# Q and K of the first two tiles on 32-column tiles of TensorE, in an adaLN transformer block on one core

## The chip, the cores and the metric

One Trainium2 chip, one of its cores. The metric is the device time of one execution in microseconds (us), lower is better. A core has TensorE (PE) for matmuls, with its weight loads shown as PEld; VectorE (DVE), ScalarE (ACT) and GpSimd (POOL) for elementwise work; and SyncE (SP), whose queue issues almost all DMAs here. Each engine runs its own instructions strictly in the order in which the program emits them.

## The reference

The input `x` has 2048 rows of 448 numbers (bf16). A vector `c` gives six modulation vectors. Then an attention over a dilated sliding window (8 keys, every second row, 16 heads of 28) and an MLP of 1792 follow, each with its own layernorm, modulation and gate:

```python
mod = (_silu(c) @ w_mod).reshape(c.shape[0], 6, 1, -1)
sa, ca, ga, sb, cb, gb = (mod[:, 0], mod[:, 1], mod[:, 2], mod[:, 3], mod[:, 4], mod[:, 5])
h = _layernorm(x) * (1 + ca) + sa
x = x + ga * _A_ref(h, A_wqkv, A_wo)          # qkv = h @ wqkv; window attention; @ wo
h = _layernorm(x) * (1 + cb) + sb
x = x + gb * _B_ref(h, B_w1, B_b1, B_w2, B_b2)  # layernorm, w1, gelu, w2
return x
```

## The kernel before, in words

**Tiles.** Even and odd rows are two independent sequences (`NS = 2`), since the window steps by two. Each is cut into 8 tiles of 128 rows, `p` = 0 to 7; a tile holds 128 even and 128 odd rows, so 256 columns once transposed. The contraction over 448 is done as three blocks of 128 and one of 64 (`KT = 4`, `KS = 64`). The blocks of 64 are run two at a time, one in the upper and one in the lower half of PE's rows.

**Stages of one tile.** `x` is loaded (`load_x`, L338). `front_ln` (L510) takes statistics of both halves on DVE (L456, L458), the reciprocal standard deviation ("rstd", L469 on POOL, or L466 and L467 on ACT), normalises on DVE (L478) into `zy`, copies a 64-wide tail, and turns the tile. For tiles 0 and 1 the turn is done by PE (`tr0`, `tr1`, L535) into PSUM; for tiles 2 to 7 it is a DMA transpose, called a turn below: `zT2` to `zT7`, L527. `affine` (L494) then applies the first modulation and writes `hT`. From `hT` come Q, K and V.

**Q and K.** For tiles 2 to 7 `natural_qk` (L614) uses `hT` as the stationary operand and the plain weight rows `wqk_st` as the moving one; the result is evicted, padded to 32 per head and turned by DMA (`tq2`, `tk2` and so on, L631). For tiles 0 and 1 `front_qk` (L580) makes Q and K directly in the turned layout, in which a head of 28 takes 32 partitions. For that `spread` (L432) first copies the weights into `Wqk` and `Wqr`, in which each head has 32 columns (the last four are the next head's first four and are not used). There are ten such copies: three full ones and two half-height ones for Q, and the same for K. The matmuls are then full ones, four heads to a matmul (L548, and L562 for the pieces of tile 0's first groups). The evictions are L609.

**Attention and the rest.** `attention` (L678) runs in 9 batches: `lt` logits (L738; `lt0_1` is the second half of batch 0), exp, mask, `pd` denominators (L760), `po` outputs (L771). `out_proj`, the second layernorm and the `mlp` follow.

**Two modulations.** The first (two vectors, `mod_cols`, L402) is needed by `affine`. The second (four vectors, `mods`, L634) is needed for the gates; it reads `wmod2`, four row blocks of `w_mod`, loaded by the line L362: blocks 0, 1 and 2 are 448 KB each, block 3 is 224 KB. Its result goes through ACT (L646) to HBM (L648) and comes back as rows (L650).

**silu(c)** is built from exp (ACT, L392), two DVE steps (L394, L395), a product on DVE (L396) and an ACT copy that repeats it 32 times (L398).

**What sets the order.** Every operation is a numbered task with an estimated cost and its dependencies (`Plan.add`, L111). The estimates are not used here: `ORDER` (L51) is a list of task numbers written out by hand, and `emit` (L140) emits them in that order, so it fixes the order of each engine's queue. A letter behind a number picks an engine (`:A` is ACT, `:P` POOL, `:D` DVE). `n+k@m` puts `k` warm-up matmuls on zeros (`filler`, L379) ahead of task `n`. `SLOTS` (L43) gives each buffer its place, in PSUM one of four.

PE can be divided into smaller arrays, by rows, by columns or both; the shape of a piece stands in the profile as `128*32` (rows by columns). A change of that division is called a change of mode below.

Of the kernel before, what the change touches and what calls it, by code (L numbers as in the profile page):

```python
# [10 lines left out]
BF16 = mybir.dt.bfloat16  # L11
# [38 lines left out]
]  # L50
ORDER = """  # L51
3 14 17 0 1 15 5 9 10 18 11 16 13 19 20 2 6 24 21 73 55+12@55 26 12 71 25 56 72 74 57 75 22 58 77 23 59 60 27 62 61 76
32 4 67 66 68+11@68 78 63 28 108 64 30 110 69 79 84:A 89:P 31 65 70 109 111 80 88:P 83 34 81 112:P 87:A 29 101+9@101
85 90:A 93:P 36 114 94+3@94 82 95 113 102 92:A 91 115:D 86 103 116 96 120:A 144 97 99 104 106 117:A 135 98 118:A 142
105 119:A 145 143 133 100 146 121 136 134 126 137 148 107 147 149:D 7 138 127 150 122 124 139 129 190 123 198 191 140
200 128 141 125 199 269 271 130 236 270 40 207 33 209 38 201 241 208 210 237 211 185 35 39 242 202 8 187 151:A 238 154
239 153 152 186 212 159 203 213 188 204 214:D 155 240 215 278 205 279 280 156 160 206 307:R 281 161 243 282 272 192
273:A 37 157 189 171 162 308:D 194 172 283 193 244 218 173 163 219 195 275 158 284 196 216 167 217 285 246 447:P 197
286 164 168 165 228 169:D 174 274 309 276:D 312 277 220 313 310 314 166 221 229 225 230 224 311 170 222:D 247 315 245
176 317 316 175 226 248 233 232 318 227 290 249 289:A 319 287:A 43 234 223 288 320 250 558:P 46 45 559 321 47 231 253  # L60
345 342 346 251 560 303 482:P 252 44 324 343 322 291 254 561 323 325 347 326 344 292 304 255 327 293 348 328 373:R 256
305 329 294 257 350 258 375 378 52 330 376 340:R 53 333 235 379 377 334 331 374 296 300 332 41 295 259 351 49 335 380
299 336 341 337 260 297 382 262 381 263 301 261 349 264 338:A 352 483 383 339 384 265 484 266 449 353 267 485 385 268
# [3 lines left out]
487 401 490 454 403 402 436 453 455 370 444 404 434 371:D 456 372 491 457 488 405 459 493 458 460 445 492 435 494 461  # L67
# [86 lines left out]
def kernel(  # L154
# [41 lines left out]
    Wqk = cst.tile([128, KT - 1, 2, H, HP], BF16, name="Wqk")  # L196
    Wqr = cst.tile([128, 2, H // 2, HP], BF16, name="Wqr")
# [25 lines left out]
    silu_bf = cst.tile([128, KT], BF16, name="silu_bf")  # L223
# [11 lines left out]
    wqk_st = sb("hm", [128, KT - 1, 2 * D + HP - DH], BF16, "wqk_st")  # L235
    wqr_st = sb("h2", [128, 2 * D + HP - DH], BF16, "wqr_st")
# [9 lines left out]
    def dconst(us, fn, writes):  # L246
        early.append(add("DVE", us, fn, writes=writes, after=[one], name="const " + writes[0]))
# [22 lines left out]
    dconst(0.06, lambda: nc.vector.memset(neg_half[:], -0.5), ["neg_half"])  # L270
# [85 lines left out]
    load_x(2, 4)  # L356
# [30 lines left out]
    def c_cols():  # L387
# [8 lines left out]
    add("DVE", 0.08, lambda: nc.vector.tensor_tensor(out=silu_bf[:], in0=e_c[:], in1=psc.t[:, 0, 0:128 * KT:128], op=ALU.mult),  # L396
        reads=["e_c"], bufs=[psc], writes=["silu"], name="silu")
    add("ACT", 0.18, lambda: nc.scalar.copy(out=silu_bc[:], in_=silu_bf[:].unsqueeze(2).to_broadcast([128, KT, HP])),  # L398
        reads=["silu"], writes=["silu_bc"], name="silu_bc")
# [32 lines left out]
    def spread(half):  # L432
        def heads(ap, h):
            return bass.AP(ap.tensor, ap.offset, [*ap.ap[:-1], [DH, h], [1, HP]])

        for ks in [[k] for k in range(KT - 1)]:
            k0, n = ks[0], len(ks)
            dst, src = (lambda k0=k0, n=n: Wqk[:, k0:k0 + n, half]), (lambda k0=k0, n=n: heads(wqk_st.t[:, k0:k0 + n, half * D:half * D + D], H))
            add("DVE", 0.06 + 0.18 * n, lambda dst=dst, src=src: nc.vector.tensor_copy(out=dst(), in_=src()), reads=[f"wqk{k}" for k in ks],
                bufs=[wqk_st], writes=[f"W{half}{k}" for k in ks], port=True, name="spread",  # L440
                alt={"ACT": (0.13 + 0.43 * n, lambda dst=dst, src=src: nc.scalar.copy(out=dst(), in_=src())),
# [521 lines left out]
```

## Time and profile before

| what | value |
|---|---|
| three runs, us | 168.0, 168.93, 170.48 (median 168.93) |
| the profiled execution, us | 169.75 |
| its span in the profile, us | 168.1 |
| PE busy in that span | 161.5 us, 96% |
| DVE, ACT, POOL busy | 115.8 us, 102.7 us, 47.7 us |

The span is what the profile sees of the execution; the 1.65 us around it are outside. A timeline row gives the start in us, the length in us, the engine, the line, the operation, output from inputs, the shapes and a count; consecutive instructions of one kind are merged. Square brackets give the idle time of the engine ahead of it and what ended it. SPq is SP's queue, with the time it took to issue. A row of a group gives busy us, the mean ns of one, and the idle time before. A row of the windows gives, for one stretch of time, its length and the busy time of PE, PEld, DVE, ACT and POOL, each with its count, then granted clock, DMA share and GB/s. A matmul's recorded length includes its way through the array, so several that overlap each show some 0.2 us more than they add.

### The profile page before, as it was taken

How to read it: one execution, taken by the hardware profiler on the slowest of the kernel's cores; microseconds unless marked ns; L12 is line 12 of the kernel's file. 1: busy time of each engine (PE TensorE's matmuls, PEld its weight loads, DVE VectorE, ACT ScalarE, POOL GpSimd, SP SyncE). 2: the span in 40 equal slices, each digit the busy share in tenths (PEclk: the TensorE clock that was granted, in tenths of full speed). 3: DMA queues.
4: the chain of work that ended last, by engine and by line, in shares of the span. 5: the costliest groups of instructions: out<-in, count | busy, mean ns of one | idle time of the engine just before them, and what ended most of it. 6: DMA issues, size and time to landing. Idle time of an engine off the chain costs nothing.

```text
span 168.1 us, 4962 instructions
## 1 busy us (share of the span) xinstructions
PE 161.5 (96%) x2126; PEld 83.4 (50%) x2126; DVE 115.8 (69%) x271; ACT 102.7 (61%) x142; POOL 47.7 (28%) x76
## 2 busy tenths in 40 slices
PE   7989989999997999999999999999999999999992
PEld 4768544345544544435565444556434455444562
DVE  6869899879899689998738877474798930400032
ACT  3368987779489954759866376956627730097300
POOL 4135252300361201269300113820003870007200
PEclk9999999999999999999999999999999999999999
DMA  5999989799997999910091000008110027110003
GB/s 153 325 335 297 168 265 134 152 201 170 221 200 182 236 150 236 169 35 0 4 139 46 4 0 0 4 0 97 35 55 0 0 43 195 49 60 0 0 0 109
DMA packets 35574, 18.78 MB, mean 112 GB/s; under 512 B 28508, under 2 KB 34593, under 8 KB 35553
## 3 DMA queue, kind: packets, MB, share of 16 engines
q1 hardware_dynamic: 35548, 18.47, 53.0%
q8 instruction: 16, 0.26, 0.7%
q14 instruction: 6, 0.04, 0.1%
q10 hardware_dynamic: 4, 0.00, 0.0%
HBM read 9.81 MB, written 1.84 MB: 69 GB/s over the span
## 4 chain that ended last, share of the span: by engine, by line
PE 81%; DMA 10%; DVE 2%; POOL 2%; issue 1%; SPq 1%; ACT 1%; POOLq 0%; DVEq 0%
PE p L883 26%; PE p L548 22%; PE pw L803 7%; PE pq L548 6%; PE p L554 4%; DMA x_all<-in_A_x_dram 4%; PE po L771 3%; PE lt L738 3%; PE pv L706 3%; PE pv L548 3%; DMA wm_st<-in_w_mod_dram 3%; DMA zT<-zy 2%; DMA kT<-zy 2%; PE pq L554 1%; PE pd L760 1%
## 5 line engine op out<-in xcount | busy, mean ns | idle before, releaser
L864 ACT ACTIVATE hm<-p,b_col 128x512 bf16<-128x512 f32 x56 | 33.9, 692 | 29.9 <-PE p L554 27.3
L883 PE MATMUL p<-w_s,hm 128*128 128x448 bf16 (+1 forms) x238 | 44.1, 342 | 0.0
L548 PE MATMUL p<-yT,w_s 128*128 128x512 bf16 x168 | 38.1, 379 | 0.0
L469 POOL TENSOR_TENSOR rs_all<-mvs,neg_half 128x2 f32<-128x2 f32 x22 | 16.7, 766 | 57.9 <-DVE mvs L458 57.8
L883 PEld LDWEIGHTS <-hm 128*128 128x128 bf16 x238 | 22.7, 98 | 19.2 <-issue 0.8
L889 DVE TENSOR_TENSOR x_all<-p,x1p 128x896 bf16<-128x896 f32 (+2 forms) x10 | 8.9, 902 | 25.9 <-PE p L883 25.9
L548 PEld LDWEIGHTS <-w_s 128*128 128x128 bf16 x168 | 15.8, 98 | 20.9 <-issue 2.9
L456 DVE BATCH_NORM_STATS2 stt<-x_all 128x6 f32<-128x448 bf16 x32 | 18.7, 610 | 1.2 <-DMA x_all<-in_A_x_dram 1.0
L745 ACT ACTIVATE et<-lt 128x928 bf16<-128x928 f32 x18 | 16.1, 947 | 5.3 <-PE lt L738 5.1
L841 POOL TENSOR_TENSOR x1p<-x_all,gbb_bc 128x448 f32<-128x448 bf16 x16 | 17.8, 1134 | 0.0
L548 PE MATMUL pq<-wqk_st,hT 128*128 128x448 bf16 x72 | 15.2, 354 | 0.6 <-DVE hT L502 0.5
L788 DVE TENSOR_TENSOR qT<-po,den 128x912 bf16<-128x912 f32 x9 | 9.9, 1104 | 7.0 <-ACT den L782 5.6
L751 DVE TENSOR_TENSOR et<-et,mask 128x928 bf16<-128x928 bf16 x18 | 11.6, 672 | 2.4 <-ACT et L745 2.4
L803 PE MATMUL pw<-wo_s,qT 128*128 128x448 bf16 x64 | 13.2, 353 | 0.0
L780 ACT ACTIVATE den<-pd 128x928 f32<-128x928 f32 x9 | 8.5, 940 | 5.8 <-PE pd L760 5.7
L819 DVE TENSOR_TENSOR h<-h,mod_bc 128x896 bf16<-128x896 bf16 x16 | 11.1, 709 | 0.3
L548 PEld LDWEIGHTS <-hT 128*128 128x128 bf16 x72 | 6.4, 98 | 7.7 <-issue 1.3
L628 ACT CAST zy<-pq 128x896 bf16<-128x896 f32 x10 | 9.0, 906 | 2.0 <-PE pq L554 1.9
L810 DVE TENSOR_TENSOR x_all<-pw,x_all 128x896 bf16<-128x896 f32 x8 | 8.7, 1088 | 1.7 <-PE pw L803 1.5
L782 ACT ACTIVATE den<-den,den_bias 128x928 f32<-128x928 f32 x9 | 9.6, 1072 | 0.2
L478 DVE TENSOR_SCALAR zy<-h,mvs,rs_all 128x448 bf16<-128x448 bf16 x16 | 6.6, 456 | 4.4 <-POOL rs_all L469 4.3
L456 DVE BATCH_NORM_STATS2 stt<-h 128x6 f32<-128x448 bf16 x16 | 9.4, 613 | 0.2
(115 smaller groups left out, 183.4 us busy)
## 6 DMA issues: line engine op xcount, KB each, us to landing
w_s<-in_B_w_dram SPq DMA_DIRECT2D x7, 224.0 KB, 4.2
out_dram<-x_all SPq DMA_DIRECT2D x7, 224.0 KB, 2.2
x_all<-in_A_x_dram SPq DMA_DIRECT2D x3, 448.0 KB, 6.0
wmod<-in_w_mod_dram SPq DMA_DIRECT2D x3, 448.0 KB, 7.0
w_s<-in_B_w_dram SPq DMA_DIRECT2D x3, 448.0 KB
wqk_st<-in_A_wqkv_dram SPq DMA_DIRECT2D x3, 225.0 KB
wm_st<-in_w_mod_dram SPq DMA_DIRECT2D x1, 672.0 KB
x_all<-in_A_x_dram SPq DMA_DIRECT2D x2, 224.0 KB, 2.6
```

The lines of the kernel that those rows point to most:

```text
L456: add("DVE", 0.53, lambda: nc.vector.bn_stats(out=stt[:, w, b, 0:6], in_=src()), reads=reads, bufs=bufs, after=early if w == b == 0 else ( ...
L469: ways = {"POOL": (0.55 + 0.17 * n, lambda: nc.gpsimd.tensor_tensor(out=r, in0=v, in1=neg_half[:, 0:n], op=ALU.pow))}
L548: nc.tensor.matmul(out(), lhsT=lhs(kt, slice(0, 128)), rhs=rhs(kt, slice(0, 128)), start=first and kt == 0, stop=not first and kt == KT - 2)
L745: exps.append(add("ACT", 0.83, lambda half=half, lt=lt: nc.scalar.activation(out=et.t[:, 2 * half:2 * half + 2].rearrange("p r m c -> p r ...
L751: nc.vector.tensor_tensor(out=ev, in0=ev, in1=mask[:], op=ALU.mult)
L782: exps.append(add("ACT", 0.96, lambda: nc.scalar.activation(out=den.t[:], in_=den.t[:], func=ACT.Exp, scale=-1.0, bias=den_bias[:]), bufs= ...
L788: nc.vector.tensor_tensor(out=qT[:, :, LEAD + q00:LEAD + q00 + 2 * WQ], in0=po.t[:, :, 0:NS * 4 * WQ].rearrange("p j (m c) -> p m j c", c=WQ),
L803: nc.tensor.matmul(pw.t[:, s, 0:D], lhsT=qT[:, KT * s + ft, LEAD + 128 * p:LEAD + 128 * p + 128], rhs=wo_s[:, ft, :], start=(ft == 0), sto ...
L819: add("DVE", 0.55, lambda vec=vec, op=op: nc.vector.tensor_tensor(out=h2.t[:], in0=h2.t[:], in1=vec.unsqueeze(1).to_broadcast([128, NS, D] ...
L841: add("POOL", 1.0, lambda n=n: nc.gpsimd.tensor_tensor(out=x1p.t[:, n, :], in0=xn(p, n), in1=gbb2_bc[:], op=ALU.add), reads=[f"x{p}", "gbb ...
L864: gelus.append(add("ACT", 0.585, lambda f=f, a=a, p1=p1s[g]: nc.scalar.activation(out=hm.t[:, f].rearrange("p n c -> p (n c)"), in_=p1.t[: ...
L883: nc.tensor.matmul(p2.t[:, n, 0:c1 - c0], lhsT=hm.t[:, f, n, q * 128:(q + 1) * 128], rhs=w2_s[:, f, c0:c1], start=(f == parts[0][0]), stop ...
```

## The change

1. `spread`, `Wqk` and `Wqr` go. `front_qk` takes its stationary operand straight from the weight rows: for each head of a group of four, a matmul with 32 columns of weights on its own 32-column strip of PE. What was one matmul is now four, on 128x32 tiles; the half-height block is eight on 64x32 tiles. The four columns too many are, as before, the next head's.
2. The weight rows are loaded with 896 columns instead of 900; the columns behind them are set to zero by two memsets on DVE.
3. silu's product and its repetition are one DVE step that writes `silu_bc` from PSUM.
4. The load of `x` for tiles 2 and 3 becomes two loads.
5. `ORDER` and `SLOTS` are new. Behind the front part (from the Q/K of tile 2 on) every engine keeps its sequence. In the front part, by engine:
   - SP before: ... x1, wqk0, wr1, wr0, wqk1, wqk2, x2 (tiles 2 and 3), x6, wv, wvr1, x4, w_mod block 1, wvr0, w_mod block 3, zT3, zT2, wo3, w_mod block 0, wo1, w_mod block 2, wo2, zT5, zT4, wo0, tq2, store of the modulation rows, tk2.
   - SP after: ... x1, wqk0, wqk1, wqk2, wr1, wr0, x2, x3, wv, wvr1, wvr0, x4, x6, zT3, zT2, w_mod block 1, w_mod block 3, wo3, w_mod block 0, wo1, w_mod block 2, wo2, zT5, zT4, wo0, tq2, store, tk2.
   - PE before: 12 warm-up matmuls, c, 11 more, first modulation, tr0, Q/K pieces of tile 0 (with 9 and 3 more warm-up ones), tr1 among them, Q/K of tile 0, Q/K of tile 1 with lt0_1 among it, v1, lt1_1, v0, lt0_0, lt1_0, Q/K of tile 2.
   - PE after: 8, 10 and 8 warm-up matmuls; four pieces of tile 0's Q/K, tr1, then the half-height blocks and the rest of tile 0, then as before.
   - ACT before: e_c, rstd of tile 0, silu_bc, two spreads, affine, two more spreads among the affine of tiles 0 and 1, evictions of tile 0, lt0_1's exp.
   - ACT after: e_c, rstd of tile 0, rstd of tile 1, affine of tiles 0 and 1, rstd of tile 3, evictions of tile 0, lt0_1's exp.
   - DVE after: e_c steps, silu_bc, normalise tile 0, tail, add_col, three of the copies for the modulation, statistics, the fourth copy, aggregate, statistics, aggregate, the sums of the modulation (L425), affine, normalise tile 1, statistics of tiles 2 and 3. Before, the two aggregates and the spreads stood behind the sums.
   - POOL after: no spreads, rstd of tiles 1 and 3 gone to ACT; the mask's memset and selects behind tile 2's tail instead of ahead of it.

```diff
-    wqk_st = sb("hm", [128, KT - 1, 2 * D + HP - DH], BF16, "wqk_st")
-    wqr_st = sb("h2", [128, 2 * D + HP - DH], BF16, "wqr_st")
+    wqk_st = sb("hm", [128, KT - 1, 2 * D + HP], BF16, "wqk_st")
+    wqr_st = sb("h2", [128, 2 * D + HP], BF16, "wqr_st")
...
+    def make_half():
+        nc.vector.memset(neg_half[:], -0.5)
+        nc.vector.memset(wqk_st.t[:, :, 2 * D:2 * D + HP - DH], 0.0)
+        nc.vector.memset(wqr_st.t[:, 2 * D:2 * D + HP - DH], 0.0)
...
-        load(lambda: nc.sync.dma_start(out=wqk_st.t[:, kt, :], in_=A_wqkv[kt * 128:kt * 128 + 128, 0:2 * D + HP - DH]), 0.62, [f"wqk{kt}"],
+        load(lambda: nc.sync.dma_start(out=wqk_st.t[:, kt, 0:2 * D], in_=A_wqkv[kt * 128:kt * 128 + 128, 0:2 * D]), 0.62, [f"wqk{kt}"],
...
-    load_x(2, 4)
+    load_x(2, 3)
+    load_x(3, 4)
...
-    add("DVE", 0.08, lambda: nc.vector.tensor_tensor(out=silu_bf[:], in0=e_c[:], in1=psc.t[:, 0, 0:128 * KT:128], op=ALU.mult),
-        reads=["e_c"], bufs=[psc], writes=["silu"], name="silu")
-    add("ACT", 0.18, lambda: nc.scalar.copy(out=silu_bc[:], in_=silu_bf[:].unsqueeze(2).to_broadcast([128, KT, HP])),
-        reads=["silu"], writes=["silu_bc"], name="silu_bc")
+    add("DVE", 0.2, lambda: nc.vector.tensor_tensor(
+        out=silu_bc[:], in0=e_c[:].unsqueeze(2).to_broadcast([128, KT, HP]),
+        in1=psc.t[:, 0, :].rearrange("p (k n) -> p k n", n=128)[:, :, 0:HP], op=ALU.mult),
+        reads=["e_c"], bufs=[psc], writes=["silu_bc"], name="silu_bc")
...
-    def spread(half):
...
-    def front_qk(u):
...
+    def front_qk(p):
+        c0 = LEAD + 128 * p
         for half in range(2):
+            pq = psum("pq")
+            done = []
+            for i in range(2):
+                state = []
+
+                def piece(kts, i=i, half=half, pq=pq, state=state):
+
+                    for kt in kts:
+                        rest, first = kt == KT - 1, not state
+                        state.append(kt)
+                        for r, a in [(r, a) for r in range(4) for a in range(2)] if rest else [(r, a) for a in range(2) for r in range(4)]:
+                            rows = slice(KS * a, KS * a + KS) if rest else slice(0, 128)
+                            w = wqr_st.t[rows] if rest else wqk_st.t[:, kt]
+                            d0 = half * D + DH * (4 * (i + 2 * a) + r)
+                            nc.tensor.matmul(pq.t[HP * r:HP * r + HP, a, NS * 128 * i:NS * 128 * (i + 1)], lhsT=w[:, d0:d0 + HP],
+                                             rhs=hT[rows, NS * kt:NS * kt + NS, c0:c0 + 128], start=first, stop=len(state) == KT,
+                                             tile_position=(rows.start, HP * r))
+
+                mine = []
+                for kts in [[kt] for kt in range(KT - 1)] if p == i == 0 else [list(range(KT - 1))]:
+                    mine.append(add("PE", 0.22 * len(kts), lambda kts=kts, piece=piece: piece(kts), reads=["wqpad"] + [f"wqk{kt}" for kt in kts] + [f"h{kt}_{p}" for kt in kts],
+                                    bufs=[pq, wqk_st], joins=[pq], after=done, mode="128x32", instr=16 * len(kts),
+                                    name=f"qk{p}_{half}{'ab'[i]}f" + (str(kts[0]) if len(kts) == 1 else "")))
+                mine.append(add("PE", 0.11, lambda piece=piece: piece([KT - 1]), reads=["wqpad", "wr0", "wr1", f"h{KT - 1}_{p}"],
+                                bufs=[pq, wqr_st], joins=[pq], after=done, mode="64x32", instr=16, name=f"qk{p}_{half}{'ab'[i]}r"))
+                done = mine
```

More of the change, by code (lines that the diff above doesn't have):

```diff
@@ L56 @@
[L56 to L60, printed above, removed]
@@ L77 @@
+650 651 659 657 665 658 668 666 669 667 676 662 663 661 677 671 660 670 680 681 684 687 683 672 678 682 675 685 673
+679 691 674 688 686 699 689 700 692 701 702 695 690 693 696 694 697 698
 """
@@ L195 @@
     kT = cst.tile([128, 4 * NS, WT], BF16, name="kT")
-    Wqk = cst.tile([128, KT - 1, 2, H, HP], BF16, name="Wqk")
-    Wqr = cst.tile([128, 2, H // 2, HP], BF16, name="Wqr")
     Wv = cst.tile([128, KT, D], BF16, name="Wv")
@@ L222 @@
     e_c = cst.tile([128, KT], FP32, name="e_c")
-    silu_bf = cst.tile([128, KT], BF16, name="silu_bf")
     silu_bc = cst.tile([128, KT, HP], BF16, name="silu_bc")
@@ L244, with dconst @@
     early = []
-    def dconst(us, fn, writes):
-        early.append(add("DVE", us, fn, writes=writes, after=[one], name="const " + writes[0]))
+    def dconst(us, fn, writes, bufs=()):
+        early.append(add("DVE", us, fn, writes=writes, bufs=bufs, after=[one], name="const " + writes[0]))
     def const(us, fn, writes, reads=()):
@@ L269 @@
     add("DVE", 0.12, make_add, writes=["add_col"], after=[one], name="add_col")
-    dconst(0.06, lambda: nc.vector.memset(neg_half[:], -0.5), ["neg_half"])
+    def make_half():
+        nc.vector.memset(neg_half[:], -0.5)
+        nc.vector.memset(wqk_st.t[:, :, 2 * D:2 * D + HP - DH], 0.0)
+        nc.vector.memset(wqr_st.t[:, 2 * D:2 * D + HP - DH], 0.0)
+    dconst(0.2, make_half, ["neg_half", "wqpad"], [wqk_st, wqr_st])
     def pads():
@@ L430 @@
     modulation()
-    def spread(half):
[L433 to L441, printed above, removed]
-                     "POOL": (0.1 + 0.5 * n, lambda dst=dst, src=src: nc.gpsimd.tensor_copy(out=dst(), in_=src()))})
-        for a in range(2):
-            rows, c0 = slice(KS * a, KS * a + KS), half * D + a * D // 2
-            src = lambda rows=rows, c0=c0: heads(wqr_st.t[rows, c0:c0 + D // 2], H // 2)
-            add("DVE", 0.22, lambda rows=rows, src=src: nc.vector.tensor_copy(out=Wqr[rows, half], in_=src()), reads=[f"wr{a}"],
-                bufs=[wqr_st], writes=[f"Wr{half}{a}"], port=True, name="spread r",
-                alt={"ACT": (0.33, lambda rows=rows, src=src: nc.scalar.copy(out=Wqr[rows, half], in_=src())),
-                     "POOL": (0.4, lambda rows=rows, src=src: nc.gpsimd.tensor_copy(out=Wqr[rows, half], in_=src()))})
     exps, lt_mms, w1_mms, gelus = [], [], [], []
     def stats(src, w, b, reads, bufs=()):
-        add("DVE", 0.53, lambda: nc.vector.bn_stats(out=stt[:, w, b, 0:6], in_=src()), reads=reads, bufs=bufs, after=early if w == b == 0 else (),
+        add("DVE", 0.53, lambda: nc.vector.bn_stats(out=stt[:, w, b, 0:6], in_=src()), reads=reads, bufs=bufs,
             writes=[f"st{w}_{b}"], name="stats")
@@ L541, in front_ln, with summed @@
             affine(u, lambda kt: ptr[kt % 2].t[:, :, kt // 2], [(ptr[0], q) for q in range(np_)], ptr, True)
-    def summed(items, slot, reads, bufs, fills, name, after=(), split=None):
+    def summed(items, slot, reads, bufs, fills, name, after=()):
         def full(first):
@@ L555, in rest @@
                                  tile_position=(rows.start, 0))
-        us = 3.5 * len(items) * slot + 0.1
-        if split:
-            for kt in range(KT - 1):
-                def piece(kt=kt):
-                    for out, lhs, rhs in items:
-                        nc.tensor.matmul(out(), lhsT=lhs(kt, slice(0, 128)), rhs=rhs(kt, slice(0, 128)), start=kt == 0, stop=False)
-                add("PE", len(items) * slot, piece, reads=reads + [f"W{name[-2]}{kt}", f"h{kt}_0"], bufs=bufs, fills=fills, after=after,
-                    instr=2 * len(items), name=f"{name}f{kt}")
-            return [add("PE", 0.5 * len(items) * slot, lambda: rest(False), reads=reads + split, bufs=bufs, fills=fills, mode="64x128",
-                       instr=2 * len(items), name=name + "r")]
         both = dict(reads=reads, bufs=bufs, joins=fills, after=after)
@@ L614, in natural_qk @@
+            dst = (kT if half else qT)[:, :, c0:c0 + 128].rearrange("p (s f) c -> p s f c", s=NS)
+            src = lambda pq=pq: pq.t[:].rearrange("p a (i s c) -> p s (a i) c", i=2, s=NS)
+            add("ACT", 0.91, lambda dst=dst, src=src: nc.scalar.copy(out=dst, in_=src()), bufs=[pq], writes=[f"{'qk'[half]}{ft}_{p}" for ft in range(4)],
+                alt={"DVE": (1.14, lambda dst=dst, src=src: nc.vector.tensor_copy(out=dst, in_=src()))}, name="evac_qk")
     def natural_qk(p):
@@ L897 @@
         front_ln(u, True)
-        if k == 0 and u[0] not in NATURAL:
-            spread(0)
-            spread(1)
         if u[0] in NATURAL:
@@ L903 @@
         else:
-            front_qk(u)
+            front_qk(u[0])
     b1_cols()
@@ L917 @@
                 else:
-                    front_qk(UNITS[i + 2])
+                    front_qk(UNITS[i + 2][0])
             if i == 0:
```

59 lines of the change are left out of this document (17 added, 42 removed), and 24 rows, old and new, of tables (ORDER, SLOTS).

## The prediction

> **What bounds the kernel now.** I read the busy time by stage first (the windows; PE is the second column of numbers, the last three are clock, DMA share and GB/s), then the chain that ended last, then the timeline of the first 34 us.
>
> ```profile
> 6.00:12.00 6.00, 5.48 (x77) 4.30 (x75) 4.89 (x24) 3.22 (x8) 2.11 (x4) 1.00 1.02 315
> ...
> 18.00:22.60 4.60, 4.21 (x129) 2.18 (x123) 3.77 (x11) 4.31 (x6) 2.29 (x3) 1.00 0.99 216
> 22.60:28.00 5.40, 5.21 (x71) 2.28 (x76) 5.33 (x16) 4.01 (x7) 1.73 (x2) 1.00 1.14 197
> ...
> 65.00:168.00 103.00, 100.07 (x1044) 49.12 (x1041) 60.17 (x117) 54.78 (x78) 29.20 (x36) 1.00 0.24 48
> ```
> From 22.6 us to the end PE is nearly full (100.07 of the last 103 us). The change leaves the order of everything after the front as it was, so the end moves by as much as the dense stretch of PE moves. What sets its start is in the chain and the timeline:
>
> ```profile
> 6.32 6.00 DMA x_all<-in_A_x_dram
> 12.34 1.68 DVE stt L456 x3
> ...
> 14.40 1.47 POOL rs_all L469 x2
> ...
> 17.17 0.29 POOL zy L490
> ...
> 17.56 3.38 DMA zT<-zy
> ...
> 30.57 3.09 DMA kT<-zy
> ```
> ```profile
> 16.12 2.74 SPq L527 DMA_TRANSPOSE zT<-zy  x2
> 21.89 0.36 PE L548 MATMUL pq<-wqk_st,hT 128*128 128x448 bf16 x1
> 22.79 2.25 PE L548 MATMUL pq<-wqk_st,hT 128*128 128x448 bf16 x11 [0.54 <-DVE hT L502]
> ```
> The load of x for tiles 2 and 3 lands at 12.32; statistics, rstd and tail follow, then the turns zT3 and zT2 (issue 16.12 and 17.5, landing of the second 20.94), the affine step, and Q/K of tile 2 at 22.79. PE's own queue was there at 21.89, did one matmul and stood 0.54 us. Two paths meet there: the turn path sets it, and the PE queue is only some 0.5 us behind. Both must move.
>
> **Turn path.** The load of tiles 2 and 3 becomes two loads of 224 KB. At the 315 GB/s of 6 to 12 us, 224 KB is 0.73 us: tile 2 should land near 11.6 and tile 3 near the old 12.3, since the bytes ahead of it are the same. One of the four statistics is then done before 12.3; three took 1.68, so one is 0.56 less. Tile 3's rstd goes from POOL (1.47 for two, 0.73 each) to ACT, two steps of about 0.2 each (my estimate from the pair in the row below): 0.3 less.
>
> ```profile
> L467 ACT ACTIVATE rs_all<-rs_all 128x2 f32<-128x2 f32 x2 | 0.4, 204 | 0.1
> ```
> So zT3 is issued some 0.9 earlier, near 15.2. The two issues take 2.74 together, so zT2 follows 1.37 later, at 16.6. The mask that stood on POOL ahead of tile 2's tail is moved behind it, which lets the tail keep this pace; on POOL it now runs where that engine sat idle, and if that cover were gone the next rstd would be late by the mask's 1.3 us (from 15.87, the end of the two rstd, to 17.17). zT2 lands about 0.95 earlier, near 20.0. Bounds: 0.3 earlier, if tile 3's x waits on the slowest transfer as before and only the rstd counts, to 1.6, if x of both lands 0.7 sooner too. I take 0.95; that alone would put the dense stretch at 21.85.
>
> **PE's queue.** The removed copies, with the work around them:
>
> ```profile
> L441 ACT COPY Wqk<-wqk_st 128x512 bf16<-128x512 bf16 x2 | 1.2, 618 | 1.1 <-DMA wqk_st<-in_A_wqkv_dram 1.1
> L439 DVE COPY Wqk<-wqk_st 128x512 bf16<-128x512 bf16 x3 | 0.9, 285 | 0.1
> ```
> ```profile
> 6.19 0.30 ACT L398 COPY silu_bc<-silu_bf 128x128 bf16<-128x128 bf16 x1 [0.61 <-DVE silu_bf L396]
> 8.07 0.15 DVE L425 TENSOR_TENSOR mod_col<-ps_col,add_col 128x8 f32<-128x8 f32 x1
> 8.60 0.73 DVE L502 TENSOR_SCALAR hT<-ptr,mod_col 128x256 bf16<-128x256 bf16 x2
> 11.05 0.39 PE L562 MATMUL pq<-hT,Wqk 128*128 128x256 bf16 x2 [0.43 <-DVE Wqk L439]
> 11.28 0.61 PE L535 MATMUL ptr<-ident,zy 128*128 128x128 bf16 x8
> ```
> ```profile
> 11.93 1.93 ACT L504 ACTIVATE hT<-ptr,mod_col 128x256 bf16<-128x256 bf16 x4 [1.10 <-PE ptr L535]
> 12.58 2.79 PE L548 MATMUL pq<-hT,Wqk 128*128 128x256 bf16 x24
> 13.74 1.02 ACT L609 CAST qT<-pq 128x1024 bf16<-128x1024 f32 x1
> 15.85 0.44 PE L738 MATMUL lt<-qT,kT 28*64 28x58 bf16 x32
> ```
> Silu: one DVE step right behind the reciprocal writes the broadcast itself. The trace has no such step; the bounds are 0.15 (the 128x8 read of PSUM at 8.07) and 0.4 (half of the two at 8.60, 128x256). I take 0.28, between them in size: it stands in the place of the copy's 0.30, and the 0.61 that ACT waited falls away, so the broadcast is ready some 0.6 earlier than 6.49. That does not reach the affine step, because the sums of the modulation (8.07) now stand on DVE behind two statistics, two aggregates and one more copy. I reckon DVE reaches the affine step at 8.85, 0.25 later than 8.60. The two memsets of the weights' pads, about 0.06 each, lie in the time in which DVE waits for x and c; uncovered they cost 0.1.
>
> First Q/K pieces: four pieces of 0.22 from about 9.3, with no wait for copies (0.43 at 11.05). Tile 1's normalise loses the copies among it on DVE, so its transposes start near 10.5 instead of 11.28, and its affine on ACT ends near 13.0 instead of 13.86. After the transposes PE has 2.2 us of tile 0's Q/K left, to about 13.6 with the changes of mode. On ACT, tile 3's rstd stands ahead of the two evictions and waits for the statistics, to about 13.95. Two evictions of 1.02 then put lt0_1 at 16.1, against 15.85: 0.25 later. What is queued behind that rstd on ACT is both evictions, and PE waits for them; this is the wait that the new order adds.
>
> The 32-column tiles: 48 full matmuls of 256 columns become 48 rounds of four, and 16 half-height ones become 8 rounds of eight. The nearest rows:
>
> ```profile
> 27.03 1.05 PE L641 MATMUL pb<-wmod,silu_bc 128*32 128x448 bf16 x16
> ```
> ```profile
> L641 PEld LDWEIGHTS <-silu_bc 128*32 128x32 bf16 x12 | 0.2, 95 | 0.4 <-issue 0.4
> ```
> ```profile
> 37.89 1.26 PE po L771 x128
> ```
> Sixteen matmuls of 448 columns in groups of four side by side take 1.05 us. One after another, at the 2.25/11 = 0.2 of the row at 22.79, they would take over 3. Four rounds in (1.05 - 0.36) / 3 = 0.23 is at most 0.03 above 0.2, one change of mode included. So a round costs between nothing and 0.04 more than one full matmul (0.11 by 2.79/24); over 48 rounds 0 to 1.9 us. Issue does not bind: 128 pairs in 1.26 us is 10 ns each, so a round of four needs 0.04, below its 0.11. I take 0.25 in all, for the two or three more mode changes that fall on the path, since most of the four early pieces fill time in which PE waited anyway. The queue reaches Q/K of tile 2 at 21.89 + 0.25 + 0.25 = 22.4 (bounds 21.6 to 24.0).
>
> The later of 21.85 and 22.4 is 22.4: **0.4 earlier** than 22.79. The fewer warm-up matmuls cost nothing while the clock column stays at 1.00.
>
> **Second modulation.** Two parts, 448 and 224 KB, move from ahead of the turns to behind them. On SP they are two more issues between zT2 and the loads of wo and the rest of w_mod.
>
> ```profile
> wmod<-in_w_mod_dram SPq DMA_DIRECT2D x1, 448.0 KB, 5.8
> ```
> ```profile
> 20.45 1.48 SPq L362 DMA_DIRECT2D wmod<-in_w_mod_dram  x1
> 24.14 2.61 SPq L527 DMA_TRANSPOSE zT<-zy  x2
> 33.71 0.70 PE L738 MATMUL lt<-qT,kT 28*64 28x58 bf16 x64 [0.36 <-DMA kT<-zy]
> ```
> The last part, issued at 20.45, landed 5.8 later, 26.25; the second modulation's matmuls ran at 27.03, so the spare time is 0.8. In the changed kernel 672 KB more must pass after the turns: 2.2 us at 315 GB/s, 3.2 at the 216 of 18 to 22.6. Against that, the turns end 0.95 earlier, and the 216 and 197 GB/s of those stretches, well under 315, say that the loads there wait for issue part of the time, so perhaps half hides. Landing 25.3 (all hidden) to 28.5 (none, at 216); I take 26.5, just ahead of 26.65, where PE now arrives. If it is late, PE stands still at that matmul, with po0, pd0, pd1 and Q/K of tile 3 queued behind it.
>
> SP next: zT5 and zT4 (24.14), the last of wo, tq2, the store of the modulation rows, tk2 (30.57). zT5 waits for DVE, which follows the turns, so it can come 0.9 earlier if SP is through its two extra issues (some 1.3 us) by then. kT then lands near 33.2 instead of 33.66, and the 0.36 that PE stood at 33.71 is partly saved. I add 0.1 to the gain.
>
> **Sum.** Against the profiled execution (169.75 us, of which 168.1 span, 1.65 around it): 0.4 + 0.1 = 0.5 less, 169.25. That execution is 0.8 above the median of the runs, 168.93, so the median becomes 168.4.
>
> **Rivals.**
> (1) *The gain is absorbed* (168.9): ACT's added rstd delays the evictions by 0.5 more, or the wait for kT at 33.71 stays where it is. For it: the two paths ahead of 22.79 lie within 0.55 us of each other, so one that stays keeps the other. Against it: the copies of these two rows alone were 2.1 us of ACT and DVE, and both paths lose some.
> (2) *Late modulation* (slower): the last part of w_mod lands after 26.65. By the 28.5 above PE stands 1.85; with the 0.4 won, 1.45 later than before: 170.4. It decides from a landing of 27.05 on. For it: the DMA share is 0.99 and 1.14 there. Against it: the low GB/s at that share. The Trainium skill ("DMA: Bandwidth & Descriptors", section "Queues, rings and completion order") says that each engine takes descriptors in ring order; by that, the later parts and then zT5 queue behind the moved 672 KB, and no run here shows it yet.
> (3) *Weight loads stand in the way on column tiles*: each of the 48 rounds pays a load of 0.095, 4.6 us in PE's queue: dense at 27.0, 4.2 later, 173.1. Against it: the four rounds at 27.03 would then have needed about 1.3 us, not 1.05. The Trainium skill ("TensorE: Matmul & The Clock Gate", "Part 3: Packing small matmuls — row/col tiling") has this rule: a weight load overlaps running matmuls only where the row group differs, and in these tiles it does not. The trace, with 1.05 us, speaks against it.
> (4) *Both paths move fully* (167.6): the queue gains too, because the evictions start at 13.4, and the dense stretch starts at 21.5.
>
> **How the numbers follow.** Forecast 0.50, (1) 0.22, (2) 0.17, (3) 0.04, (4) 0.07. The likeliest gives 168.4. The runs of before lie from 168.0 to 170.48, so a median may stray by some 0.7. The range goes from 166.9, which is (4) less 0.7, to 170.5, which is (2). A measurement of this kernel can tell about 2%, 3.4 us: faster than 165.5 needs more than any case gives (0.03); slower than 172.3 is (3) and a knock-on of (2) into zT5 (0.05); within 2% is the rest, 0.92.
>
> **What would show it.** Right: zT's first issue near 15.2, lt0_1 near 16.1, Q/K of tile 2 without a wait on hT at about 22.4, no wait on w_mod at the second modulation, kT landing before PE needs it. Each step wrong: x of tile 3 still landing at 12.3 with DVE idle beyond it; ACT standing before tile 3's rstd while PE waits for kT of tile 0; rounds of four at over 0.15 us; PE waiting for w_mod near 26.7. The prediction is wrong if the dense stretch starts after 23, or if what it won is lost by 34 us.

## The result, and the profile after

| | before | after |
|---|---|---|
| median of the runs, us | 168.81 (6 runs, 168.0 to 170.48) | 174.22 (6 runs, 172.61 to 177.4) |
| the profiled execution, us (its span) | 169.75 (168.1) | 174.17 (172.4) |
| start of TensorE's dense stretch (Q/K of tile 2), us | 22.79 | 26.96 |
| first MLP matmul, us | 64.2 | 68.7 |

The changed kernel is slower: ratio 1.0268, 95% interval [1.0215, 1.0322]. (Medians are over all executions; the ratios, here and below, leave out those more than 1.5% above the fastest of the same kernel, so the two can differ, and the profiles of e9 and e10 below are of executions left out in this way.) The forecast was 168.4, with a range of 166.9 to 170.5. The span grew by 4.3 us, and the dense stretch starts 4.2 us later, so the loss lies ahead of it, in the front.

The chain that ended last, after (start, length, what). "issue" is time in which TensorE waited for nothing that the profile shows:

```profile
8.48 1.03 PE pq L384 x8
9.51 0.99 PE pq L566 x32
10.50 0.55 PE ptr L517 x8
11.05 3.19 PE pq L566 x113
14.25 2.43 issue
16.67 2.59 PE pq L566 x63
...
25.31 0.50 PE lt L708 x42
25.81 0.91 issue
26.72 0.31 PE lt L708 x16
27.03 2.38 PE pq L530 x12
```

Before, the chain up to 22.79 ran through loads, DVE, POOL and the turns. Now it is TensorE itself from 8.48 on, with two stretches of idle time that have no releaser: 2.43 us in the middle of a group of tile 1's Q/K matmuls, where no operand is missing, and 0.91 us inside the logits of a later batch. The timeline after, around the first:

```profile
10.43 0.62 PE L517 MATMUL ptr<-ident,zy 128*128 128x128 bf16 x8
...
11.32 1.93 PE L566 MATMUL pq<-hT,wqk_st 128*32 128x256 bf16 x64
...
13.53 0.72 PE L566 MATMUL pq<-hT,wqk_st 128*32 128x256 bf16 x17
13.67 1.01 ACT L580 CAST kT<-pq 128x1024 bf16<-128x1024 f32 x1
...
14.88 2.72 SPq L509 DMA_TRANSPOSE zT<-zy  x2
...
16.67 0.40 PE L566 MATMUL pq<-hT,wqk_st 128*32 128x256 bf16 x7 [2.43 <-issue]
```

17 of a group's 24 matmuls are done, then nothing, then the other 7 follow. The windows after show what the pause does to the clock (third number from the end), and how many matmuls and weight loads were recorded up to three of these pauses (the two counts behind PE and PEld):

```profile
12.00:18.00 6.00, 3.57 (x120) 2.34 (x112) 5.86 (x18) 3.35 (x7) 2.07 (x7) 0.96 0.70 196
18.00:22.60 4.60, 4.60 (x122) 2.87 (x115) 2.65 (x10) 2.35 (x3) 2.25 (x3) 0.68 1.17 212
```
```profile
0.00:15.50 15.50, 12.28 (x223) 8.53 (x223) 13.12 (x63) 7.35 (x16) 2.65 (x15) 1.00 0.83 260
0.00:26.50 26.50, 21.41 (x478) 13.88 (x479) 19.22 (x81) 12.76 (x22) 6.49 (x25) 0.94 0.89 244
0.00:43.50 43.50, 37.51 (x862) 22.03 (x862) 33.05 (x108) 27.12 (x41) 9.01 (x28) 0.96 0.89 204
```

446, 957 and 1724 instructions: 511 and 767 apart, which is 2 and 3 times 256 less one each. With a few instructions that the windows don't count (waits, drains), the pauses stand behind TensorE's instructions 449, 961 and 1729. In the runs below, too, the pauses of over 0.5 us behind the first 10 us for which no view names a releaser stand behind instruction 449 + 256 k, with two exceptions that stay unexplained: 0.80 us at 58.02 in e5 (behind 2188) and 0.66 us at 63.20 in e10 (behind 2130), both in `po` matmuls. The profile's page also lists a queue named "instruction":

```profile
q8 instruction: 18, 0.29, 0.7%
```

Before it had 16 packets and 0.26 MB: one packet of 16 KB for 256 instructions. The trace lists 4263 TensorE instructions before and 4631 after; counted from 193 in steps of 256, that makes 16 and 18 edges, as many as packets. TensorE recorded 2126 matmuls before and 2309 after. In the DMA view of the changed kernel from 10.1 to 14.1 us, no packet of q8 moves and the data fill the engines; from 14.1 to 15.5, with the loads done, one does:

```profile
q1 hardware_dynamic: 1096, 1.36, 101.4%
```
```profile
q1 hardware_dynamic: 57, 0.09, 16.3%
q8 instruction: 1, 0.02, 4.8%
```

**Theory.** TensorE's instructions come by DMA in blocks of 256. The next block's packet moves some time after a block is entered, later when loads stand in the DMA engines, and TensorE stops if it has used up its block before the packet has landed and some 1.4 us more have passed. (Behind 961 the packet had landed at 25.28, the block was used up at 25.62, and TensorE went on at 26.72.) A 32-column tile costs a matmul and a weight load for a quarter of the work, so a block of them is gone in some 4 us. **Rivals:** that column tiles or their weight loads are slow in themselves; that the later modulation loads or the new order of turns cost the time; that the missing warm-up matmuls do.

### The profile page after: what moved, and what is told of

The parts are those of the page before. It is cut to its first block, busy times and chain, and to the rows that moved or that the text cites. A ratio compares the mean times of both kernels' runs of the same rounds, so it can differ in the third digit from the quotient of the medians.

```text
span 172.4 us, 5322 instructions
## 1 busy us (share of the span) xinstructions
PE 162.5 (94%) x2309; PEld 83.7 (49%) x2309; DVE 114.9 (67%) x270; ACT 101.0 (59%) x141; POOL 44.9 (26%) x71
## 4 chain that ended last, share of the span: by engine, by line
PE 84%; DMA 4%; issue 4%; DVE 4%; ACT 2%; POOL 0%; DVEq 0%
PE p L853 25%; PE p L530 22%; PE pq L530 7%; PE pw L773 5%; PE pq L566 5%; PE pv L676 5%; PE p L536 4%; PE lt L708 4%; DMA yT<-zy 3%; PE po L741 2%; DMA x_all<-in_A_x_dram 2%; PE pq L536 1%; PE pv L530 1%; DVE stt L438 1%; PE pd L730 1%
## 5 line engine op out<-in xcount | busy, mean ns | idle before, releaser
L451 POOL TENSOR_TENSOR rs_all<-mvs,neg_half 128x2 f32<-128x2 f32 x20 | 15.2, 763 | 69.4 <-DVE mvs L440 69.4
L853 PEld LDWEIGHTS <-hm 128*128 128x128 bf16 x238 | 22.7, 98 | 19.2 <-issue 0.8
L530 PEld LDWEIGHTS <-w_s 128*128 128x128 bf16 x168 | 15.8, 98 | 21.6 <-issue 3.8
L721 DVE TENSOR_TENSOR et<-et,mask 128x928 bf16<-128x928 bf16 x18 | 10.9, 635 | 7.5 <-ACT et L715 7.5
L566 PE MATMUL pq<-hT,wqk_st 128*32 128x256 bf16 x192 | 7.5, 304 | 2.4 <-issue 2.4
```

The source lines that it names most:

```text
L451: ways = {"POOL": (0.55 + 0.17 * n, lambda: nc.gpsimd.tensor_tensor(out=r, in0=v, in1=neg_half[:, 0:n], op=ALU.pow))}
L530: nc.tensor.matmul(out(), lhsT=lhs(kt, slice(0, 128)), rhs=rhs(kt, slice(0, 128)), start=first and kt == 0, stop=not first and kt == KT - 2)
L566: nc.tensor.matmul(pq.t[HP * r:HP * r + HP, a, NS * 128 * i:NS * 128 * (i + 1)], lhsT=w[:, d0:d0 + HP], rhs=hT[rows, NS * kt:NS * kt + NS, ...
L721: nc.vector.tensor_tensor(out=ev, in0=ev, in1=mask[:], op=ALU.mult)
L853: nc.tensor.matmul(p2.t[:, n, 0:c1 - c0], lhsT=hm.t[:, f, n, q * 128:(q + 1) * 128], rhs=w2_s[:, f, c0:c1], start=(f == parts[0][0]), stop ...
```

## The experiments

Measured marks of all runs. The lags are from the first instruction of a block to the landing of the packet that it brings, for the blocks entered behind instructions 193 and 449, and the pauses are from the last start before to the first start behind an edge (so some 0.2 longer than "issue"); both are worked out from the trace's list of TensorE instructions and of q8's packets. Waits with a named releaser are left out. Pauses of up to 0.3 need not be a matter of blocks: at e8's 0.28 and at both of e12's, the packet had landed some 5 us or more before. The start of Q/K of tile 2 is read from the timeline or from the chain, which differ by up to 0.07.

| run | lags, us | pauses at block edges up to 60 us (behind instruction) | Q/K of tile 2 | first MLP matmul | ratio to before |
|---|---|---|---|---|---|
| before | 4.5, 2.2 | 1.04 (1729), 0.21 (1985) | 22.79 | 64.2 | 1 |
| after | 5.2, 2.7 | 2.70 (449), 1.10 (961), 1.41 (1729) | 26.96 | 68.7 | 1.0268 |
| e1 | 2.7, 1.9 | 0.62 (705), 0.49 (1729) | 23.57 | 66.3 | 1.0455 |
| e2 | 3.4, 3.1 | 0.25 (705), 0.63 (961), 0.91 (1729), 0.28 (2497) | 23.00 | 66.6 | 1.013 |
| e3 | 3.5, 4.3 | none | 21.79 | 65.1 | 1.0108 |
| e4 | 2.2, 3.8 | 2.74 (705), 1.21 (1729) | 25.90 | 67.4 | 1.0273 |
| e5 | 4.9, 2.7 | 0.94 (449) | 22.56 | 64.7 | 1.0171 |
| e6 | 3.4, 2.4 | 0.20 (449), 1.39 (1473) | 23.69 | 65.5 | 1.0123 |
| e7 | 1.5, 1.1 | 1.15 (1729) | 30.16 | 71.7 | 1.0546 |
| e8 | 2.6, 3.6 | 0.55 (449), 2.39 (705), 0.28 (1473), 0.79 (1729) | 27.62 | 68.7 | 1.0365 |
| e9 | 1.9, 1.5 | 1.17 (1729) | 28.25 | 72.2 | 1.0418 |
| e10 | 3.3, 0.9 | 0.20 (449) | 27.05 | 70.2 | 1.0271 |
| e11 | 2.3, 3.4 | 1.10 (1473) | 25.26 | 66.5 | 1.0149 |
| e12 | 3.1, 3.8 | 0.30 (961), 0.19 (1217) | 22.61 | 64.8 | 1.0161 |

**e1_fewer_warm**: the changed kernel with 8 warm-up matmuls fewer.

```diff
-... 83 92+8@92 32 104 ...
+... 83 92 32 104 ...
```

> The changed kernel without the 8 warm-up matmuls ahead of the first Q/K piece: 16 PE instructions fewer, the same program otherwise. Theory A (PE runs out of instructions: they come in blocks of 256, and a block that is fetched late stops PE at a fixed count of instructions, 449 here): the gap of about 2.4 us stays behind recorded instruction 449, so it moves 8 weight-load and matmul pairs further into tile 1's first Q/K group, from 17 of its 24 pairs done to all 24 done and one of the next group; time within 1 us of 174.2. Theory B (a wait that belongs to the program, such as a transfer or an eviction that the records do not name): the gap stays behind 17 of the 24 pairs. Theory C (weight loads are not hidden on column tiles): rounds of four would take over 0.15 us, here as in the changed kernel, and the gap has no say; nothing moves.

176.79 us, ratio 1.0455 [1.0362, 1.0548]. A miss in the place: nothing stood behind 449. The packet landed 2.7 after the block was entered instead of 5.2, so Q/K of tile 2 began at 23.57. The clock fell to 0.77 from 6 to 12 us, and the time went elsewhere: 1.96 us of "issue" at 89.18, again at a block's edge (behind 3265), deep in a stage that the change doesn't touch, with the clock at 0.84 from 92 to 100 us.

**e2_more_tiny**: the changed kernel, with 65 matmuls of 16 columns in the opening in place of 5 warm-up matmuls.

```diff
-... 56+8@56 ... 63+10@63 ...
+... 56+6@56 ... 63+7@63 ...
...
+        for _ in range({"c_cols": 20, "mod_cols": 45}.get(t.name, 0)):
+            nc.tensor.matmul(t.sums[0].t[:, 0, 0:16], lhsT=warm_w[:, 0:128], rhs=warm_w[:, 0:16], start=True, stop=True)
```

> The changed kernel with 65 very short matmuls (16 columns, on zeros) added among the early warm-up ones and 5 of the long warm-up ones left out: 120 PE instructions more before the first Q/K piece. Theory A: the second block is entered near 6 us, before most of the loads are queued, so the next block is fetched earlier; the gap of 2.4 us in tile 1's Q/K goes, and a smaller one, about 1 us, comes near lt0_1 at 16 us, where PE waits anyway; 171 to 172.5 us, faster although instructions were added. Theory B: the gap stays where it is and the time is 174 to 175.

171.77 us, 1.013 [1.0052, 1.0207]: with 120 TensorE instructions more it is 2.4 us faster than the change, as expected. The edges now fall at other work, and no pause reaches 1 us. So it is not the number of instructions that counts but where a block runs out.

**e3_before_wmod_late**: the kernel before with only the modulation loads moved behind the turns.

```diff
-... 83 34 81 ... 93:P 36 114 ... 200 128 141 125 ...
+... 83 81 ... 93:P 114 ... 200 128 141 34 36 125 ...
```

> The kernel before with one thing changed: w_mod blocks 1 and 3 are loaded behind the turns zT3 and zT2. Theory A: PE's instructions are as few as before, no new gap; 168.2 to 169.5, the same as before. A rival in which the late second modulation is what costs (PE waits for w_mod near 27 us and kT comes late): 170 to 172, with PE standing ahead of the second modulation's matmuls.

170.48 us, 1.0108 [1.0062, 1.0154]: 1.5 us, above the 168.2 to 169.5 that the theory alone had let expect and in the rival's range. The timeline of this run shows rival (2) of the prediction, the wait for `w_mod` at the second modulation, and the next turns, which took 5.17 to issue instead of the 2.61 of before:

```profile
23.11 5.17 SPq L527 DMA_TRANSPOSE zT<-zy  x2
...
26.56 0.56 PE L641 MATMUL pb<-wmod,silu_bc 128*32 128x448 bf16 x8 [0.27 <-DMA wmod<-in_w_mod_dram]
...
28.36 0.67 PE L641 MATMUL pb<-wmod,silu_bc 128*32 128x448 bf16 x8 [1.24 <-DMA wmod<-in_w_mod_dram]
```

The Trainium skill ("DMA: Bandwidth & Descriptors", "Queues, rings and completion order") says that each engine takes descriptors in ring order. The turns held up behind the moved 672 KB (5.17 against 2.61) agree with it.

**e4_after_wmod_early**: the changed kernel with those loads ahead of the turns again.

```diff
-... 103 33 84 ... 115 35 260 226 197 37 120 ...
+... 103 33 35 37 84 ... 115 260 226 197 120 ...
```

> The changed kernel with w_mod blocks 1 and 3 loaded ahead of the turns again, as before the change. Theory A with its second half (the fetch is late because it queues behind the loads that are under way): 672 KB more are queued at 10 to 14 us, so the gap at instruction 449 does not shrink and may grow by up to 2 us; 173.5 to 176. If the moved w_mod were the cause of the loss: back to 169 to 170.

173.47 us, 1.0273 [1.0218, 1.0329]. The pause moved on by one block, and was as long; it had been expected to stay behind 449. There the packet landed 2.2 us after its block was entered, not 5.2, although the DMA view shows the data at 104.5% from 9.9 to 12.3 us. So full engines alone don't make a packet late; what else decides is open. In the chain:

```profile
16.11 0.99 PE pq L566 x32
17.10 2.47 issue
19.57 0.98 PE pq L566 x16
```

So the late modulation explains nothing of the change's loss: with TensorE late, it was hidden (after the change the second modulation started at 31.4 and waited for no load).

**e5_half_column**: the changed kernel, with Q and K of tile 1 on full matmuls from spread copies. **e6_half_column_mod_early**: the same with the modulation loads early.

```diff
+    Wqk = cst.tile([128, KT - 1, 2, H, HP], BF16, name="Wqk")
+    Wqr = cst.tile([128, 2, H // 2, HP], BF16, name="Wqr")
...
+                        for a in range(2) if p else ():
+                            ... one matmul of 128 columns from Wqk or Wqr
+                        if p:
+                            continue
```

> The changed kernel, with the Q and K of tile 1 (not of tile 0) on full matmuls from spread copies again; the copies go to POOL (8) and ACT (2). TensorE gets 192 instructions fewer than in the changed kernel. The theory of instruction supply: the dense matmuls of the opening use up their 256-instruction blocks more slowly, so the idle time without a named releaser behind instructions 449, 705 or 961 falls from 2.4 us to 1.6 or less, and the start of Q and K of tile 2 from 26.96 to 24 to 25.5. The time is then 169.5 to 172, since the late loads of the modulation weights are still in it. The rival, that moving the modulation loads or the earlier turns costs the 4 us by themselves: the time stays at 173 to 175, and tile 2 starts at 26.5 or later.

> As the run before, with the two modulation blocks ahead of the turns again, as in the kernel before. The theory of instruction supply, with the late modulation loads as a second cost that shows only when TensorE isn't late: 168.3 to 170, level with the kernel before. The rival (the late modulation costs nothing by itself): the same time as the run before this one. If the one-step silu and the missing copies on the vector engine gain something that the column tiles took away, it shows here as a time below 168.

e5: 170.75 us, 1.0171 [1.0083, 1.0259]. e6: 170.32, 1.0123 [1.0036, 1.021]. e5 is in the range of the theory, with tile 2 earlier than the 24 to 25.5 expected; e6 lies 0.3 us above its range, and its interval leaves it slower than the kernel before. (e6's profile also has the clock at 0.72 from 6 to 12 us.) The chain of e5:

```profile
13.51 1.85 PE pq L588 x16
15.36 0.87 issue
16.23 0.39 PE pq L588 x4
...
22.56 2.42 PE pq L553 x12
...
29.99 4.41 DMA kT<-zy
```

With 192 instructions fewer the pause is 0.87 and tile 2 starts at 22.56, ahead of the kernel before; the transposed K then lands later than before (34.40 against 33.66), so the lead is lost. Whether the modulation loads make a difference here isn't decided: the intervals of e5 and e6 overlap. Neither beats the kernel before.

**e7_loads_behind_turns**: the changed kernel with four loads behind the turns.

```diff
-... 98 29 67 ... 69 31 101 ... 102 30 81 ... 103 33 84 ... 190 131 113 ...
+... 98 67 ... 69 101 ... 102 81 ... 103 84 ... 190 131 29 31 30 33 113 ...
```

> The changed kernel with the loads of the V weights and of tile 6 and 7's input (four transfers) moved behind the turns of tiles 3 and 2, so that fewer loads are in the queues at 8 to 14 us. If the instruction packets for TensorE wait in the DMA engines behind loads: the packet behind instruction 449 lands by 13 instead of 15.2, the stretch of 2.4 us without a named releaser shrinks to under 1, and the time is 170 to 171.5. If the packet's time doesn't hang on the loads: the stretch stays at 2 to 2.7 at the same place and the time at 173 to 175.

177.35 us, 1.0546 [1.0476, 1.0615]. The mechanism came out, the time didn't. From 11.2 to 13.0 us the DMA view of this run, and then its windows from 11.2 to 15.6:

```profile
q1 hardware_dynamic: 58, 0.09, 12.7%
q8 instruction: 1, 0.02, 3.6%
```
```profile
11.20:15.60 4.40, 4.40 (x144) 3.15 (x136) 2.96 (x10) 2.66 (x7) 0.70 (x1) 0.92 0.08 27
```

With a DMA share of 0.08 the packet landed at 12.69, 1.5 after its block was entered, and the next one 1.1 after: TensorE ran all its column tiles through without a pause. The time was lost to a moved load, the weights of V, at whose first matmul TensorE stood; behind that wait the clock was at 0.50 from 22.6 to 28 us. The chain has it:

```profile
18.80 4.54 DMA Wv<-in_A_wqkv_dram
...
23.38 2.97 PE pv L676 x15
```

**e8_before_column_tiles**: the kernel before, with the column tiles alone.

```diff
+                    for r in range(4) if strips else ():
+                        nc.tensor.matmul(out()[HP * r:HP * r + HP], lhsT=lhs(kt, slice(0, 128))[:, HP * r:HP * r + HP], rhs=rhs(kt, slice(0, 128)),
+                                         start=first and kt == 0, stop=not first and kt == KT - 2, tile_position=(0, HP * r))
+                    if strips:
+                        continue
...
```

> The kernel before, with one part of the change alone: each matmul of Q and K of tiles 0 and 1 becomes four matmuls on 32-column tiles, from the spread copies, which are still made; loads, turns, silu and copies stay as they were. TensorE gets 384 instructions more and the same matmul columns at four at a time. The theory of instruction supply: idle stretches without a named releaser behind instructions 449, 705 or 961, together 1.5 to 4 us, the start of Q and K of tile 2 at 24 to 26.5 instead of 22.79, and 170.5 to 173.5 us. The rival, that the column tiles cost nothing by themselves and the new order of loads and turns does it all: 168.3 to 169.6, with tile 2 at 22.8.

174.5 us, 1.0365 [1.0281, 1.0449]: this part alone costs 5.9 us, above the range that was expected. The chain of this run, then its window behind the pause:

```profile
14.10 1.64 PE pq L550 x56
15.75 0.28 issue
16.02 1.27 PE pq L550 x40
...
18.23 0.77 PE pq L550 x24
19.00 2.12 issue
21.12 1.47 PE pq L550 x20
...
27.62 2.43 PE pq L554 x12
```
```profile
18.00:22.60 4.60, 2.48 (x81) 1.70 (x68) 3.08 (x11) 1.85 (x2) 1.94 (x3) 0.82 1.23 178
22.60:28.00 5.40, 5.40 (x131) 2.78 (x132) 2.43 (x8) 3.77 (x5) 0.60 (x2) 0.84 0.45 154
```

Loads, turns, copies and silu are those of before, so the rivals that lay it on these fall. That the tiles are slow in themselves falls too: 56 of them, 14 rounds of four, took 1.64, which is 0.117 a round. What is added is 2.12 + 0.28 of pauses and, at clocks of 0.82 and 0.84, 4.60 x 0.18 + 5.40 x 0.16 = 1.7 us of slower matmuls behind them: 4.1 of the 4.8 us by which tile 2 starts later than before.

**e9_x6_behind_turns**: the changed kernel with one load moved. **e10_half_column_x6_behind**: e5 with the same.

```diff
-... 103 33 84 ... 190 131 113 ...
+... 103 84 ... 190 131 33 113 ...
```

> The changed kernel with only one load, the 448 KB of input of tiles 6 and 7, moved behind the turns, and the V weights left where they were. If TensorE's instruction packets wait behind queued loads: the packet behind the block that is entered at 10.3 lands at 13.5 to 14.5 instead of 15.56, the stretch behind instruction 449 falls from 2.7 to 0.6 to 1.7, and the time to 171.5 to 173.5, since nothing waits for V's weights this time. If a stretch moves to instruction 705 or 961 instead, the time stays at 173 to 174.5 and the sum of the stretches is as before. If the packet doesn't hang on the loads: no change in either.

> The changed kernel with Q and K of tile 1 on full matmuls from spread copies, and the input of tiles 6 and 7 loaded behind the turns. Instruction supply: no stretch over 0.5 behind 449, Q and K of tile 2 start at 21.5 to 22.5, ahead of the kernel before (22.79), and then it is the modulation weights (about 26.5 to 28) and the transposes of K behind the moved loads that set the pace: 169.5 to 171. If the later transfers cost nothing, it is below 168.5 and beats both kernels.

e9: 177.0 us, 1.0418 [1.0312, 1.0523]. e10: 173.63, 1.0271 [1.0173, 1.037]. Both are above the expected ranges. (The times in e9's expectation count from a point 0.3 us earlier than the profile's views.) In both the lags fell and no pause of over 0.2 is left in the front; but a new wait took its place, which neither expectation had. DVE's statistics of that tile stand in its queue ahead of tile 2's affine step, and now they wait for the moved load; tile 2 then starts at 27 to 28. In e9's timeline:

```profile
24.74 1.15 DVE L438 BATCH_NORM_STATS2 stt<-x_all 128x6 f32<-128x448 bf16 x2 [5.61 <-DMA x_all<-in_A_x_dram]
```

**e11_before_edges_moved**: the kernel before, with the 65 small matmuls of e2 for 5 warm-up ones (12 to 10, and 11 to 8). **e12_half_column_edges_moved**: e6 with the same edit as in e2.

> The kernel before with its useful work untouched: 5 of the warm-up matmuls of 256 columns are dropped and 65 matmuls of 16 columns take their place in the opening, so that every 256-instruction block of TensorE ends 120 instructions earlier in the work. Instruction supply: the one stretch of the kernel before that stands at a block's edge (1.04 behind instruction 1729, at 51.17) goes or shrinks below 0.4, since that edge now falls elsewhere, and unless another edge falls badly the time is 167.3 to 168.5. If the stretch at 51 isn't a matter of blocks, it stays where it is in the work, and the time is 168.3 to 169.5.

> The kernel of the sixth run (Q and K of tile 1 on full matmuls, the modulation loads ahead of the turns) with the same 65 small matmuls for 5 warm-up matmuls. Its stretch of 1.39 behind instruction 1473 and that of 0.20 behind 449 change place, since the work at the edges is other work. Instruction supply: 168.5 to 170 if no edge falls in the column tiles of tile 0 while loads are queued, 170 to 171.5 if one does; in either case every stretch without a releaser stands behind instruction 193 + 256 k. The rival, that the stretches belong to the work: they stay at the same matmuls, 170.3 as in that run.

e11: 171.89 us, 1.0149 [1.0089, 1.0209]. e12: 171.92, 1.0161 [1.0102, 1.022]. Moving the edges moves the pauses. The chain of e11 has one in the `po` matmuls, where before had none:

```profile
40.01 1.07 PE po L773 x124
41.08 0.91 issue
41.99 0.21 PE po L773 x4
```

The pause that the kernel before has in the logits is gone, as the theory says. In the chain of before it stands as

```profile
50.57 0.48 PE lt L738 x43
51.05 0.85 issue
51.90 0.34 PE lt L738 x18
```

But the hoped-for time didn't come, in either: e11's turns landed at 23.49 instead of 20.94, and e12 has 1.30 us of "issue" at 117.85, behind instruction 4033 = 449 + 14 x 256, in the MLP. No version tried beats the kernel before.

## Why the prediction was wrong, point by point

**The step that failed** is "Issue does not bind: 128 pairs in 1.26 us is 10 ns each, so a round of four needs 0.04, below its 0.11", and with it the arrival of TensorE's queue at Q/K of tile 2 at 22.4, with bounds of 21.6 to 24.0. It arrived at 26.96. The 10 ns are right inside a block; what the sum lacked is how fast new blocks come. In the changed kernel the block entered at 10.0 was used up at 14.0, and its successor's packet landed at 15.2; TensorE went on at 16.7, 1.4 after the landing. The kernel before spent 7.8 us on the block entered at 11.6, and the packet, with a lag of 4.5, was in time. The terms now add up, from the chain and the windows quoted above: 22.4 as predicted, 2.43 and 0.91 for the two pauses, 4.60 x 0.32 = 1.5 and 6.00 x 0.04 = 0.2 for the lower clock: 27.4, against 26.96. The 22.4 wasn't measured by itself, and the 0.4 too much is open.

A hint was in the trace of before, in the idle 0.85 us at 51.05 without a releaser and in the 16 packets of the queue named "instruction"; the prediction used neither. The Trainium skill ("Runtime: NRT & Kernel Launch", "Instruction fetch mechanics") says that instructions come in blocks of 256 through a DMA queue, and that crossing a block is mostly hidden. The runs agree with the blocks and not with the second part: 2.43 us here, 2.12 in e8.

**The clock.** "The fewer warm-up matmuls cost nothing while the clock column stays at 1.00" held by its wording, but the column fell to 0.68. That fall came behind the pause: in the trace it is one stretch at 0.50, from 17.5 to 20.9 us. A like stretch of about 3.4 us begins within 1 us of the end of the pauses of 2.47 (e4), 2.12 (e8) and 1.96 (e1, at 89.18), and none behind those of 0.87 (e5), 1.20 (e6) and 1.30 (e12). The warm-ups aren't cleared by this. e5 has as many as the changed kernel and a clock of 1.00 in all windows of the front, but the profiles of e6, e7 and e10, with as many, show 0.72 from 6 to 12 us and that of e1, with fewer, 0.77, with no such pause ahead of it; before, e3 and e8, with the warm-ups of before, show 1.00 there. In e7 the first 32 column matmuls took 1.90 us by this, not 1.06. So in the changed kernel's profile the fewer warm-ups cost nothing that shows, but they can; what that is worth wasn't tried by itself.

**Right.** Rounds of four on column tiles cost no more than one full matmul: 16 rounds in the row `11.32 1.93`, so 0.12, and rival (3), a weight load of 0.095 for each, is refuted. That its price put the dense stretch at 27.0 is chance; the time was lost in two places, not in each round. zT3 was issued at 14.88 (predicted 15.2), tile 1's transposes started at 10.43 (10.5), and ACT's first eviction at 13.67, earlier than the 13.95 that was feared.

**The turn path was wrong too**, though it decided nothing here. Issued 1.24 us earlier, the turns still landed no earlier. The timeline after has the affine step at 20.98, waiting for them; before, it started at 21.04:

```profile
20.98 1.25 DVE L484 TENSOR_SCALAR hT<-zT,mod_col 128x512 bf16<-128x512 bf16 x3 [1.95 <-DMA zT<-zy]
```

That zT2 would land near 20.0 failed, since the second turn, issued at 16.34, took 4.5 to land in place of the 3.4 that it took before (17.56 to 20.94). So even with TensorE's queue on time, tile 2 would have started near 22.7 (20.98 and the 1.75 that lay between the two before), as it did in e5 (22.56) and e12 (22.61): rival (1), no gain.

**Late modulation** did not show in the changed kernel, since TensorE came even later. e3 shows it alone: TensorE stood 0.27 + 1.24 = 1.51 us for `w_mod` (the rival's worst case had 1.85), and the time rose by 1.5, near the rival's 1.45. That the two sums meet is partly luck, since e3's dense stretch starts 1.0 us earlier than before (21.79), not 0.4, and the late turns behind took the rest.

## What to carry to other kernels

A matmul on a quarter of the array costs the same two instructions as one on the whole array, so count TensorE's instructions by blocks of 256 and set the time in which a block is used up (here 4.0 us on column tiles, 7.8 before) against the time in which the next one lands while loads are in flight (up to 5.7 us here), and 1.4 us more. Idle time without a releaser in the middle of a group of like matmuls, at instruction counts that differ by multiples of 256, is the mark of it, and the price is the pause and, behind the pauses of about 2 us and more, the lower clock. Edits far ahead, even to warm-up matmuls, move the edges and can make or remove pauses everywhere behind them, so a part of a change is best tried alone (e8) before its savings are added up.

## What the runs showed of the hardware that was not expected

- An instruction packet's lag hangs on the loads, but not on them alone: 1.5 and 1.1 us with the DMA engines nearly idle (e7), 5.2 and 4.5 with loads queued (after, before), and 2.2 with the engines just as full (e4). The longest up to 60 us is 5.7, from 45.0 to 50.7 in the kernel before, ahead of its pause. From the landing to TensorE's next start it took another 1.2 to 2.0 us wherever TensorE had paused for the packet by over 0.5 us, 1.4 to 1.6 in the changed kernel.
- Turns seem slower when such a packet falls among them. In e3, where no packet moved between issue and landing, the second turn took 3.13 us; in e11, with a packet from 20.5 to 21.6 among them, 5.40; in e12, 4.94. This is seen side by side only and wasn't tried by itself, and it can't be all: a later turn of e12, issued at 35.05 with no such packet among its transfers, took 4.7.
